# The product of w3 and w_out2 moved between two feed-forwards, its tiles converted in the middle blocks, and the sign merged into a parametric ReLU

## The chip, the core and the metric

The kernel runs on one core of a Trainium2 chip. The metric is the device time of one execution in microseconds, lower is better. TensorE (PE) multiplies, ScalarE (ACT) and VectorE (DVE) work on tiles, GpSimd (POOL) only fills constants here, and SyncE (SP) issues every DMA.

## The reference

A chunked attention is followed by two feed-forwards over 3072 tokens of 512 features:

```
x = attention(q, k, v, mem_k, mem_v)   # chunks of 32 queries, 64 keys each
x = elu(x @ w_in) @ w_out              # w_in 512x2048, w_out 2048x512
h = ((x @ w1) * (x @ w2)) @ w3         # w1, w2 512x1024, w3 1024x1024
out = h @ w_out2                       # w_out2 1024x512
```

q, k and v are float32; the weights are float64 and reach the chip as pairs of 32-bit words.

## The kernel before

Nothing stands between w3 and w_out2, so their product WC (1024x512) is made once on the chip, and the second feed-forward ends in one matmul by WC. Every matmul of the feed-forwards and of WC is done as three (`mm3`, lines 121 to 123), with each operand split into a high half and the rest: a `split` is one cast on ScalarE (line 117) and one subtraction on VectorE (line 118).

**Conversion.** A float64 tile of 128x512 (512 KB) becomes float32 on the chip in a job. `rebase` (line 155, ScalarE) scales the high word as if it were a float32, which moves the exponent. `shift` (159), `sign` (163) and `low` (169) are VectorE instructions on the bits: three places left, the sign put back, the top bits of the low word joined. Then the tile is split into one of 32 weight slots `W`. `Feed.step` issues one stage of each of several jobs, so that one call is about one job's worth of instructions; the letter f in the order strings stands for it. Raw tiles come through four buffers, and at the start through six more that lie where six of the slots will be. There are 72 jobs: 16 of w3, 8 of w_out2, 16 of w_in, 16 of w_out, 8 each of w1 and w2.

**Attention.** 24 groups of 128 queries pass through `plan`, steps 0 to 9: transposes of q and k (`at_turn`, `at_turn2`), scores, maximum and exponential, sum, norm, a flip on VectorE, values, and `at_out`, which splits the result into `xhl`, the input of the first feed-forward. A group begins every 32/3 steps. `at_step`, the letter a, issues the next step. All of it uses the two PSUM banks `PA`. `load_qk` for the next group is issued in step 1 and `load_v` in step 9, on SyncE's queue like every other DMA.

**The order.** It is written out by hand, and each engine executes its instructions in that order. `START` and the loop behind it mix the first 31 attention steps (three groups) with the jobs of w3, w_out2 and w_in 0 to 7 and with the matmuls of WC (`mm_wc`); a job of w3 has two more stages, four transposes on TensorE (`flip`, line 425) and a split from PSUM. WC is stored to DRAM (`wcd`). Then come eight blocks of 384 tokens. A block has 16 iterations of `mm_h` (12 matmuls), `elu_exp` (ReLU and exponential on ScalarE, lines 391 and 392), `mm_x` of two iterations before (12 matmuls), and `elu_split` (lines 398, 117, 118), with two attention steps of the next block's groups in each. In block 0 the rest of the jobs of w_in and w_out stand between them by `IN_BLOCK0`, three steps in two iterations. Blocks 1 to 6 hold no conversion. Block 7 holds no attention, but from its fourth iteration on one conversion step each, for w1 and w2, into slots that the block sets free. The result x1 of a block goes to DRAM (`x1d`) through the tiles `f` and comes back, split, for the second feed-forward.

The second feed-forward has eight blocks of eight iterations: `mm_ab` (24 matmuls), a product on VectorE, and `mm_o` of the iteration before (9 matmuls of 512 columns). In its first block it also finishes the conversion of w1 and w2 and loads a tile of WC per iteration.

Of the kernel before, what the change touches and what calls it, by code (L numbers as in the profile page):

```python
# [19 lines left out]
def tile_kernel(  # L20
# [68 lines left out]
    wcd = [dram.tile([P, 2, DM], F32, name=f"wcd{i}") for i in range(FF2)]  # L89
# [82 lines left out]

    class Job:
        def __init__(self, load, *phases):
            self.load, self.phases = load, ((rebase,), (shift, low), (sign,)) + phases

    class Feed:
# [3 lines left out]
        def __init__(self, jobs, ahead=lambda at: RAWS):  # L181
            self.jobs, self.at, self.loaded, self.ahead = jobs, 0, 0, ahead

        def load(self, n):
            while self.loaded < min(len(self.jobs), n):
                job = self.jobs[self.loaded]
                fn, *args = job.load
                job.raw = fn(*args)
# [12 lines left out]
        def until(self, i):  # L201
            while self.at - len(self.jobs[i].phases) < i:
                self.step()

    def to_slot(slot):
        def fn(job):
            t = W[slot]
            split(t[:, 0, :], t[:, 1, :], job.f)

        return fn  # L210
# [143 lines left out]
    def at_out(G):  # L354
# [6 lines left out]

    plan = [
        (0, at_turn), (1, at_turn2), (1, lambda G: load_qk(G + 1)), (2, at_scores), (3, at_max), (4, at_sum),
        (5, at_norm), (6, at_flip), (8, at_values), (9, at_out), (9, lambda G: load_v(G + 1)),
    ]
    steps = [[] for _ in range(AT_BEFORE + AT_BLOCK * NB)]
    for G in range(NG):
        for at, fn in plan:
            steps[AT_BLOCK * G // GPB + at].append((fn, G))
# [47 lines left out]
    NW3 = 5  # L417
    S_WO2, S_W3T, S_WC = 2 * FF1 - FF2, FF1 - NW3, (FF1 + 3, 2 * FF1 - FF2)

    def wc_job(half, c):  # L420
        slot = S_W3T + (half * FF2 + c) % NW3

        def flip(job):
            for i in range(KT):
                nc.tensor.transpose(PS[4 + c % 2][:, i * P:(i + 1) * P], job.f[:, i * P:(i + 1) * P], ident)

        def back(job):
            t = W[slot]
            split(t[:, 0, :], t[:, 1, :], PS[4 + c % 2])

        return Job((raw_cols, w3[half * KT * P:(half + 1) * KT * P, :], c), (flip,), (back,))

    def mm_wc(half, c, i):
        t, x = W[S_W3T + (half * FF2 + c) % NW3], W[S_WO2 + c]
        ii = slice(i * P, (i + 1) * P)
        mm3(PS[i], t[:, 0, ii], t[:, 1, ii], x[:, 0, :], x[:, 1, :], c == 0, c == FF2 - 1)

    def store_wc(half, i):
        t = W[S_WC[half] + i]
        split(t[:, 0, :], t[:, 1, :], PS[i])  # L440
        stores.append((wcd[half * KT + i], t))

    stores = []

    def store_next():
        if stores:
            o, t = stores.pop(0)
            nc.sync.dma_start(out=o, in_=t.bitcast(F32))
# [49 lines left out]
    with tc.manual_schedule():  # L498
        def weight(i):
            if i < FF1:  # L500
                return Job((raw_cols, w_in, i), (to_slot(i),))
            return Job((raw_rows, w_out, i - FF1, 0), (to_slot(i),))
# [33 lines left out]
        for half in range(2):  # L536
            for c in range(FF2):
# [4 lines left out]
                elif c == SPARE_END:  # L542
                    end_more()
# [122 lines left out]
```

## Time and profile before

| | |
|---|---|
| median of 3 runs | 1182.76 us (1182.22 to 1183.58) |
| the profiled execution's own time | 1183.67 us |
| its span in the trace | 1181.9 us |
| TensorE busy | 1104.5 us, 93% |
| VectorE busy | 532.5 us, 45% |
| ScalarE busy | 435.8 us, 37% |
| DMA moved | 91.06 MB, mean 77 GB/s |

Busy shares are means over the whole span; the stages differ, so they are read stage by stage. Matmuls are pipelined, and a matmul's recorded duration is longer than its distance to the next, so distances between starts are used for TensorE, and for short instructions of the other engines too.

### The profile page before, as it was taken

What the parts mean: (1) busy time and instruction counts of PE and PEld (TensorE: products, weight loads), DVE (VectorE), ACT (ScalarE), POOL (GpSimd) and SP (SyncE); (2) the same over time, 40 slices, a digit from 0 to 9 for tenths busy, and PEclk for the clock granted to TensorE, in tenths of its full rate; (3) what the DMA queues carried; (4) which work ended last, traced back from release to release, by engine and by line L of the source; (5) the groups of instructions that cost most, each with busy time, mean ns of one, the idle gap of its engine ahead of it and who ended that gap; (6) DMA issues with size and microseconds to landing.
All of it is one profiled execution on the core that took longest, in us unless ns stands there. A gap on an engine that the chain in (4) does not pass through costs nothing.

```text
span 1181.9 us, 20762 instructions
## 1 busy us (share of the span) xinstructions
PE 1104.5 (93%) x8800; PEld 1033.9 (87%) x8800; DVE 532.5 (45%) x984; ACT 435.8 (37%) x897; POOL 3.0 (0%) x16
## 2 busy tenths in 40 slices
PE   4768787899999999999999999889999999999998
PEld 3546677899999999999999999889999999999997
DVE  4989778545444444444344445653212212221221
ACT  3554455344434444444335335532212212121211
POOL 1000000000000000000000000000000000000000
PEclk9999888999999999999999999999999999999999
DMA  8955574221221222112212123332100001000000
GB/s 256 279 171 184 152 206 123 54 47 37 63 46 42 72 47 62 37 35 64 52 36 73 25 77 126 129 129 104 54 27 27 28 26 54 24 31 28 1 27 27
DMA packets 143165, 91.06 MB, mean 77 GB/s; under 512 B 102113, under 2 KB 134881, under 8 KB 143073
## 3 DMA queue, kind: packets, MB, share of 16 engines
q1 hardware_dynamic: 143072, 89.74, 26.3%
q8 instruction: 69, 1.13, 0.4%
q14 instruction: 24, 0.19, 0.1%
HBM read 72.94 MB, written 16.78 MB: 76 GB/s over the span
## 4 chain that ended last, share of the span: by engine, by line
PE 78%; DVE 11%; ACT 5%; issue 3%; DMA 2%; SPq 0%; POOL 0%; ACTq 0%; POOLq 0%; DVEq 0%
PE bank L121 21%; PE bank L123 20%; PE bank L122 20%; PE banks L123 4%; PE banks L122 4%; PE banks L121 4%; DVE f L169 2%; PE banks L352 2%; DVE f L163 2%; DVE w L118 2%; DVE f L159 1%; PE banks L294 1%; ACT w L117 1%; ACT eg L392 1%; ACT eg L391 1%
## 5 line engine op out<-in xcount | busy, mean ns | idle before, releaser
L121 PE MATMUL bank<-xhl,w 128*128 128x384 f32 x768 | 266.7, 347 | 5.6 <-DVE eg L398 5.6
L123 PE MATMUL bank<-xhl,w 128*128 128x384 f32 x768 | 260.8, 340 | 0.0
L122 PE MATMUL bank<-xhl,w 128*128 128x384 f32 x768 | 260.6, 339 | 0.0
L117 ACT CAST g<-eg 128x384 fp32r<-128x384 f32 x192 | 98.7, 514 | 287.1 <-DVE eg L398 146.6
L121 PE MATMUL bank<-g,w 128*128 128x384 f32 x512 | 176.3, 344 | 2.8 <-ACT g L117 2.8
L122 PE MATMUL bank<-g,w 128*128 128x384 f32 x512 | 172.6, 337 | 0.3 <-DVE g L118 0.2
L123 PE MATMUL bank<-g,w 128*128 128x384 f32 x512 | 172.4, 337 | 0.0
L118 DVE TENSOR_TENSOR g<-eg,g 128x384 fp32r<-128x384 f32 x192 | 107.2, 558 | 141.7 <-ACT g L117 141.7
L121 PEld LDWEIGHTS bank<-xhl,w 128*128 128x128 f32 x768 | 146.5, 191 | 13.4 <-DVE eg L398 7.8
L479 DVE TENSOR_TENSOR eg<-eg,banks 128x384 f32<-128x384 f32 x64 | 35.5, 555 | 259.0 <-PE banks L123 259.0
L122 PEld LDWEIGHTS bank<-xhl,w 128*128 128x128 f32 x768 | 146.7, 191 | 2.7
L123 PEld LDWEIGHTS bank<-xhl,w 128*128 128x128 f32 x768 | 146.7, 191 | 0.0
L391 ACT ACTIVATE eg<-bank 128x384 f32<-128x384 f32 x128 | 62.8, 490 | 173.9 <-PE bank L123 173.3
L398 DVE SCALAR_TENSOR_TENSOR eg<-eg,bank 128x384 f32<-128x384 f32 x128 | 69.8, 545 | 74.6 <-ACT eg L392 74.6
L121 PEld LDWEIGHTS bank<-g,w 128*128 128x128 f32 x512 | 97.2, 190 | 5.0 <-ACT g L117 3.4
L122 PEld LDWEIGHTS bank<-g,w 128*128 128x128 f32 x512 | 97.3, 190 | 0.8 <-DVE g L118 0.8
L123 PEld LDWEIGHTS bank<-g,w 128*128 128x128 f32 x512 | 97.0, 189 | 0.0
L478 ACT COPY eg<-bank 128x384 f32<-128x384 f32 x64 | 30.8, 481 | 165.6 <-PE bank L123 165.6
L121 PE MATMUL banks<-xhl,w 128*128 128x384 f32 x256 | 85.6, 334 | 0.0
L123 PE MATMUL banks<-xhl,w 128*128 128x384 f32 x256 | 85.5, 334 | 0.0
L122 PE MATMUL banks<-xhl,w 128*128 128x384 f32 x256 | 85.5, 334 | 0.0
L121 PE MATMUL bank<-w,g 128*128 128x512 f32 x192 | 74.8, 390 | 1.4 <-DMA w<-wcd 1.4
(70 smaller groups left out, 1344.4 us busy)
## 6 DMA issues: line engine op xcount, KB each, us to landing
raw<-in_moe_w_dram SPq DMA_DIRECT2D x24, 512.0 KB
raw<-in_moe_w_out_dram SPq DMA_DIRECT2D x20, 512.0 KB
raw<-in_moe_w_in_dram SPq DMA_DIRECT2D x13, 512.0 KB
qn<-in_q_dram SPq DMA_DIRECT2D x24, 256.0 KB
x1d<-st SPq DMA_DIRECT2D x32, 192.0 KB
x<-x1d SPq DMA_DIRECT2D x32, 192.0 KB
out_dram<-st SPq DMA_DIRECT2D x24, 256.0 KB
kn<-in_k_dram SPq DMA_DIRECT2D x20, 256.0 KB
```

The lines of the kernel that those rows point to most:

```text
L117: nc.scalar.copy(hi, src)
L118: nc.vector.tensor_tensor(out=lo, in0=src, in1=hi.bitcast(F32), op=ALU.subtract)
L121: mm(o, lhsT=w_hi, rhs=x_hi, start=start, stop=False)
L122: mm(o, lhsT=w_hi, rhs=x_lo, start=False, stop=False)
L123: mm(o, lhsT=w_lo, rhs=x_hi, start=False, stop=stop)
L163: nc.vector.scalar_tensor_tensor(out=t, in0=h, scalar=-(2 ** 31), in1=t, op0=ALU.bitwise_and, op1=ALU.bitwise_or)
L169: nc.vector.scalar_tensor_tensor(out=t, in0=l, scalar=29, in1=t, op0=ALU.logical_shift_right, op1=ALU.bitwise_or)
L352: mm(o, lhsT=vw[cc, u, 2 * hp + r, :], rhs=pT[cc, r, hp, u, :], start=u == 0, stop=u == 1)
L391: nc.scalar.activation(e, h_t[n], AF.Relu, scale=-1.0)
L398: nc.vector.scalar_tensor_tensor(out=e, in0=e, scalar=-1.0, in1=ph, op0=ALU.add, op1=ALU.max)
L478: nc.scalar.copy(e, pab[0])
L479: nc.vector.tensor_tensor(out=e, in0=e, in1=pab[1], op=ALU.mult)
```

## The change

The jobs of w3, w_out2, w1 and w2 leave the start and block 7. The start now holds the first 31 attention steps and twelve conversion steps, for w_in and w_out alone; block 0 has two steps in each iteration as long as there are any. From group 6 on, each of the 18 remaining attention groups carries one or two jobs of w_out2, w1 and w2, and the first 16 of them also one of w3: rebase, shift and low, and split, in steps of their own. A w3 tile is transposed into `PA` in step 9. Each split tile is stored to DRAM as high and low halves, 512 KB, by the next `at_step`. In block 7 each slot that a matmul has read for the last time is filled again from DRAM, 32 fills; eight more follow during the product. WC is made between the two feed-forwards, 192 matmuls without conversion among them, and stays in slots. `sign` is gone: the rebase is a parametric ReLU with a slope of 2^32 for negative inputs, so that the bit which the shift moves to the top carries the sign. A step now issues high half, shift and low of the next tile, low half, rebase. `at_out` moves from step 9 to step 8. The queries and keys are loaded ahead of the first weights.

```diff
-    RAWS, SPARE, SPARE_JOBS, SPARE_END = 4, (8, 9, 10, 16, 17, 18), 27, 5
-    START = "llikflfafafffafa"
-    IN_WC = (("", "a", "f", "af"), ("f", "a", "f", "a"))
-    AFTER_WC = ("afaa", "aaa")
-    IN_BLOCK0 = (("fa", "a", "f"), ("af", "a", ""))
+    RAWS, SPARE, SPARE_JOBS, SPARE_END = 4, (13, 14, 15, 29, 30, 31), 20, 22
+    START = "ikllll" + 3 * "aafaafaafaafa"
+    IN_BLOCK0 = ("fa", "fa", "")
...
-    wcd = [dram.tile([P, 2, DM], F32, name=f"wcd{i}") for i in range(FF2)]
+    w3d = [[dram.tile([P, 2, 512], F32, name=f"w3d{h}_{c}") for c in range(FF2)] for h in range(2)]
+    wod = [dram.tile([P, 2, 512], F32, name=f"wod{c}") for c in range(FF2)]
+    wabd = [[dram.tile([P, 2, 512], F32, name=f"wabd{c}_{r}") for r in range(2)] for c in range(FF2)]
...
-        nc.scalar.activation(job.f, job.raw[:, :, 1].bitcast(F32), AF.Copy, scale=2.0 ** -112)
+        nc.scalar.activation(job.f, job.raw[:, :, 1].bitcast(F32), AF.Prelu, scale=2.0 ** -112, alpha=2.0 ** 32)
...
-    def sign(job):
-        h, t = job.raw[:, :, 1], job.f.bitcast(I32)
-        nc.vector.scalar_tensor_tensor(
-            out=t, in0=h, scalar=-(2 ** 31), in1=t, op0=ALU.bitwise_and, op1=ALU.bitwise_or
-        )
...
+    def hi_of(job, src=None):
+        nc.scalar.copy(job.to[:, 0, :], job.f if src is None else src)
+    def lo_of(job, src=None):
+        nc.vector.tensor_tensor(
+            out=job.to[:, 1, :], in0=job.f if src is None else src, in1=job.to[:, 0, :].bitcast(F32), op=ALU.subtract
+        )
...
-        def step(self, n=1):
-            for _ in range(n):
-                self.load(self.at + 1)
-                for age, op in ((5, 0), (4, 0), (3, 0), (1, 0), (2, 0), (1, 1), (0, 0)):
-                    i = self.at - age
-                    if 0 <= i < len(self.jobs) and age < len(self.jobs[i].phases):
-                        self.jobs[i].phases[age][op](self.jobs[i])
-                self.at += 1
-                self.load(self.at - 2 + self.ahead(self.at))
+        def do(self, i, *ops):
+            if 0 <= i < len(self.jobs):
+                for op in ops:
+                    op(self.jobs[i])
+        def step(self):
+            i = self.at
+            if i == SPARE_END:
+                end_more()
+            self.load(i + 1)
+            if 0 <= i - 2 < len(self.jobs):
+                self.jobs[i - 2].to = W[self.jobs[i - 2].slot]
+            self.do(i - 2, hi_of)
+            self.do(i - 1, shift, low)
+            self.do(i - 2, lo_of)
+            self.do(i, rebase)
+            self.at += 1
+            self.load(i + RAWS + (len(SPARE) if i + len(SPARE) + RAWS <= SPARE_JOBS else 0))
...
+    mid_jobs, mid_loaded, stores = [], [0], []
+    def mid_load(n):
+        while mid_loaded[0] < min(len(mid_jobs), n):
+            mid_jobs[mid_loaded[0]].fetch()
+            mid_loaded[0] += 1
+    def mid_low(job):
+        shift(job)
+        low(job)
+        mid_load(mid_jobs.index(job) + 3)
+    def mid_split(job, src=None):
+        job.to = pools["st"].tile([P, 2, 512], F32R, tag="st", name="st")
+        hi_of(job, src)
+        lo_of(job, src)
+        stores.append(job)
+    def mid_flip(job):
+        for i in range(KT):
+            nc.tensor.transpose(PA[:, 0, i * P:(i + 1) * P], job.f[:, i * P:(i + 1) * P], ident)
+        mid_split(job, PA[:, 0, :])
+    def store_next():
+        while stores:
+            job = stores.pop(0)
+            nc.sync.dma_start(out=job.store, in_=job.to.bitcast(F32))
     plan = [
         (0, at_turn), (1, at_turn2), (1, lambda G: load_qk(G + 1)), (2, at_scores), (3, at_max), (4, at_sum),
-        (5, at_norm), (6, at_flip), (8, at_values), (9, at_out), (9, lambda G: load_v(G + 1)),
...
+    others = [Job((raw_rows, w_out2, c, 0), store=wod[c]) for c in range(FF2)]
+    others += [Job((raw_cols, (w1, w2)[r], c), store=wabd[c][r]) for c in range(FF2) for r in range(2)]
+    w3s = [Job((raw_cols, w3[h * KT * P:(h + 1) * KT * P, :], c), store=w3d[h][c]) for h in range(2) for c in range(FF2)]
...
+        if G >= GM:
+            n = [(G - GM + i) * n_others // (NG - GM) for i in range(2)]
+            for job, at in zip([others.pop(0) for _ in range(n[1] - n[0])], (0, 6)):
+                mid_jobs.append(job)
+                for i, fn in enumerate((rebase, mid_low, mid_split)):
+                    steps[s0 + at + i].append((fn, job))
+                if at == 0 and w3s:
+                    job = w3s.pop(0)
+                    mid_jobs.append(job)
+                    for at3, fn in ((4, rebase), (5, mid_low), (9, mid_flip)):
+                        steps[s0 + at3].append((fn, job))
...
     def at_step():
         if at_done[0] < min(at_most[0], len(steps)):
+            store_next()
             for fn, G in steps[at_done[0]]:
                 fn(G)
             at_done[0] += 1
...
-    def wc_job(half, c):
-        slot = S_W3T + (half * FF2 + c) % NW3
-        def flip(job):
-            for i in range(KT):
-                nc.tensor.transpose(PS[4 + c % 2][:, i * P:(i + 1) * P], job.f[:, i * P:(i + 1) * P], ident)
-        def back(job):
-            t = W[slot]
-            split(t[:, 0, :], t[:, 1, :], PS[4 + c % 2])
-        return Job((raw_cols, w3[half * KT * P:(half + 1) * KT * P, :], c), (flip,), (back,))
...
+    def wc_bank(half, i):
+        return PS[i] if half else (PS[4], PS[5], PA[:, 0, :], PA[:, 1, :])[i]
...
+    def keep_wc(half, i):
+        s_wc.append(s_w3[half, i])
+        t = W[s_wc[-1]]
+        split(t[:, 0, :], t[:, 1, :], wc_bank(half, i))
+    def fill(slot, src):
+        nc.sync.dma_start(out=W[slot].bitcast(F32), in_=src)
...
-        jobs = []
-        for c in range(FF2):
-            jobs += [wc_job(0, c), Job((raw_rows, w_out2, c, 0), (to_slot(S_WO2 + c),))]
-        for c in range(FF2):
-            jobs += [wc_job(1, c), weight(c)]
-        due = {}
-        order = sorted(range(FF2, 2 * FF1), key=lambda i: i if i < FF1 else i - FF1 + 2)
+                return Job((raw_cols, w_in, i), slot=i)
+            return Job((raw_rows, w_out, i - FF1, 0), slot=i)
+        jobs, due = [], {}
+        order = sorted(range(2 * FF1), key=lambda i: i if i < FF1 else i - FF1 + 2)
         for i in order:
             due[i] = len(jobs)
             jobs.append(weight(i))
...
         run(START)
-        for half in range(2):
-            for c in range(FF2):
-                lead = min(1, 2 * c + 8 * half)
-                feed.until(2 * (half * FF2 + c) + lead)
-                if half == 0:
-                    feed.until(2 * c + 1 + lead)
-                elif c == SPARE_END:
-                    end_more()
-                store_next()
-                last = c == FF2 - 1
-                for i in range(KT):
-                    mm_wc(half, c, i)
-                    if last:
-                        store_wc(half, i)
-                    if not last:
-                        run(IN_WC[half][i])
-                if last:
-                    run(AFTER_WC[half])
...
+                store_next()
+                mid_ctx.close()
                 at_ctx.close()
                 late = ctx.enter_context(tc.tile_pool(name="late", bufs=1, side="right"))
-                pools["raw"] = ctx.enter_context(tc.tile_pool(name="raw2", bufs=RAWS, side="right"))
-                freed = []
-                for m in range(FF1 + 2):
-                    freed += [m] if m < FF1 else []
-                    freed += [FF1 + m - 2] if m >= 2 else []
-                s_ab, s_wc, jobs = {}, [], []
-                for c in range(FF2):
-                    for r, src in enumerate((w1, w2)):
-                        s_ab[c, r] = freed.pop(0)
-                        jobs.append(Job((raw_cols, src, c), (to_slot(s_ab[c, r]),)))
-                    s_wc.append(freed.pop(0))
-                feed = Feed(jobs)
+                ab_jobs = [(c, r) for c in range(FF2) for r in range(2)]
...
+                mid_ctx = ExitStack()
+                pools["raw"] = mid_ctx.enter_context(tc.tile_pool(name="raw2", bufs=2, side="right"))
+                pools["st"] = mid_ctx.enter_context(tc.tile_pool(name="st_p", bufs=2, side="right"))
+                mid_load(2)
...
                 if j == 0:
-                    run(IN_BLOCK0[f % 2][0])
+                    run(IN_BLOCK0[0])
                 else:
                     at_step()
-                    if j == NB - 1 and f >= 3:
-                        feed.step()
...
                 if j == 0:
-                    run(IN_BLOCK0[f % 2][1])
+                    run(IN_BLOCK0[1])
...
-                run(IN_BLOCK0[f % 2][2])
-            if j == 0 and f >= 3:
-                store_next()
+                run(IN_BLOCK0[2])
+            if n >= NH - FF1:
+                free = [f] if n < NH else []
+                if n >= NH - FF1 + 2:
+                    free.append(FF1 + n - 2 - (NH - FF1))
+                for slot in free:
+                    if len(s_wo) < FF2 and len(s_wo) <= len(s_w3):
+                        fill(slot, wod[len(s_wo)])
+                        s_wo.append(slot)
+                    elif len(s_w3) < 2 * FF2:
+                        half, c = divmod(len(s_w3), FF2)
+                        fill(slot, w3d[half][c])
+                        s_w3[half, c] = slot
+                    else:
+                        c, r = ab_jobs.pop(0)
+                        fill(slot, wabd[c][r])
+                        s_ab[c, r] = slot
...
+        store_x1(NB - 1)
+        for half in range(2):
+            for c in range(FF2):
+                for i in range(KT):
+                    mm_wc(half, c, i)
+                    if c == FF2 - 1:
+                        keep_wc(half, i)
+            for i in range(KT, FF2):
+                c, r = ab_jobs.pop(0)
+                fill(s_w3[half, i], wabd[c][r])
+                s_ab[c, r] = s_w3[half, i]
...
-            if j == 0 and f < FF2:
-                feed.until(2 * f + 1)
             if n < NA:
                 mm_ab(n)
-                if j == 0:
-                    nc.sync.dma_start(out=W[s_wc[f]].bitcast(F32), in_=wcd[f])
-                    feed.step()
```

## Rows read from the trace of the kernel before

**Rows 1.** Windows: engines' busy us by stage, granted clock, DMA share, GB/s.
```profile
0.00:113.50 113.50, 72.66 (x676) 55.15 (x677) 92.15 (x172) 52.83 (x96) 2.99 (x16) 0.95 0.76 226
113.50:231.70 118.20, 94.24 (x829) 89.25 (x827) 85.19 (x158) 59.60 (x124) 0.00 (x0) 0.88 0.46 131
231.70:701.30 469.60, 468.06 (x4820) 448.94 (x4819) 210.58 (x391) 197.30 (x425) 0.00 (x0) 1.00 0.20 49
701.30:772.90 71.60, 65.84 (x364) 63.09 (x363) 43.69 (x82) 36.94 (x75) 0.00 (x0) 0.99 0.44 144
772.90:1181.90 409.00, 403.67 (x2120) 377.50 (x2118) 100.87 (x185) 89.12 (x183) 0.00 (x0) 1.00 0.12 41
```

**Rows 2.** Waits of TensorE in 0 to 113.5: us in total, times, longest.
```profile
PE bank L425 <- DVE f L163: 25.8, 10, 5.4
PE banks L267 <- DMA qn<-in_q_dram: 10.7, 1, 10.7
```

**Rows 3.** Timeline of ScalarE, block 0: first and last of its 16 line-391 ReLUs.
```profile
115.82 0.49 ACT L391 ACTIVATE eg<-bank 128x384 f32<-128x384 f32 x1 [0.71 <-PE bank L123]
...
219.44 0.48 ACT L391 ACTIVATE eg<-bank 128x384 f32<-128x384 f32 x1
```

**Rows 4.** Timeline of ScalarE, block 7: ReLUs without, then with a conversion step.
```profile
713.30 0.49 ACT L391 ACTIVATE eg<-bank 128x384 f32<-128x384 f32 x1 [1.98 <-PE bank L123]
...
717.46 0.49 ACT L391 ACTIVATE eg<-bank 128x384 f32<-128x384 f32 x1 [1.98 <-PE bank L123]
...
746.95 0.48 ACT L391 ACTIVATE eg<-bank 128x384 f32<-128x384 f32 x1
...
751.68 0.48 ACT L391 ACTIVATE eg<-bank 128x384 f32<-128x384 f32 x1
```

**Rows 5.** Timeline of VectorE: one conversion step's instructions at the start.
```profile
42.56 0.68 DVE L118 TENSOR_TENSOR w<-f,w 128x512 fp32r<-128x512 f32 x1
43.16 0.42 DVE L159 TENSOR_SCALAR f<-f 128x512 int32<-128x512 int32 x1
43.49 0.68 DVE L163 SCALAR_TENSOR_TENSOR f<-raw,f 128x512 int32<-128x512 int32 x1
44.09 0.68 DVE L169 SCALAR_TENSOR_TENSOR f<-raw,f 128x512 int32<-128x512 int32 x1
44.70 0.42 DVE L159 TENSOR_SCALAR f<-f 128x512 int32<-128x512 int32 x1
```

**Rows 6.** Groups by line and form, VectorE's two ELU instructions: busy, mean ns.
```profile
L118 DVE TENSOR_TENSOR g<-eg,g 128x384 fp32r<-128x384 f32 x192 | 107.2, 558 | 141.7 <-ACT g L117 141.7
L398 DVE SCALAR_TENSOR_TENSOR eg<-eg,bank 128x384 f32<-128x384 f32 x128 | 69.8, 545 | 74.6 <-ACT eg L392 74.6
```

**Rows 7.** Windows: the stretch of the first three attention groups, all engines.
```profile
12.70:104.70 92.00, 64.07 (x637) 48.01 (x637) 80.80 (x151) 45.34 (x85) 0.00 (x0) 0.94 0.76 233
```

**Rows 8.** Groups by line and form, ScalarE: the rebase, and the table load.
```profile
L155 ACT ACTIVATE f<-raw 128x512 f32<-128x512 f32 x57 | 38.4, 674 | 17.2 <-DMA raw<-in_moe_w_out_dram 5.9 <-DMA raw<-in_moe_w_dram 4.2 <-DVE f L169 3.6
L155 ACT ACT_TABLE_LOAD x1 | 1.3, 1283 | 0.7 <-PEq L650 0.7
```

**Rows 9.** Timeline of TensorE: four transposes of w3, then product matmuls.
```profile
100.71 0.66 PE L425 MATMUL bank<-ident,f 128*128 128x128 f32 x4 [0.68 <-DVE f L163]
101.12 0.47 PE L121 MATMUL bank<-w,w 128*128 128x512 f32 x1
101.43 0.39 PE L122 MATMUL bank<-w,w 128*128 128x512 f32 x1
...
103.72 0.39 PE L123 MATMUL bank<-w,w 128*128 128x512 f32 x1
```

**Rows 10.** Windows of VectorE: the first attention group (clock, DMA share, GB/s last).
```profile
12.70:42.10 29.40, 24.49 (x47) 0.94 0.99 324
```

**Rows 11.** Timeline of SyncE: output stores of the second feed-forward's first two blocks.
```profile
830.95 1.54 SPq L495 DMA_DIRECT2D out_dram<-st  x3
...
881.08 1.53 SPq L495 DMA_DIRECT2D out_dram<-st  x3
```

More of the change, by code (lines that the diff above doesn't have):

```diff
@@ L171, in low, with __init__, fetch @@
         )
-    class Job:
-        def __init__(self, load, *phases):
-            self.load, self.phases = load, ((rebase,), (shift, low), (sign,)) + phases
+    def hi_of(job, src=None):
[4 more added lines that the diff above has]
+        )
+    class Job:
+        def __init__(self, load, slot=None, store=None):
+            self.load, self.slot, self.store = load, slot, store
+        def fetch(self):
+            fn, *args = self.load
+            self.raw = fn(*args)
@@ L177, in tile_kernel, with __init__ @@
     class Feed:
-        def __init__(self, jobs, ahead=lambda at: RAWS):
-            self.jobs, self.at, self.loaded, self.ahead = jobs, 0, 0, ahead
+        def __init__(self, jobs):
+            self.jobs, self.at, self.loaded = jobs, 0, 0
         def load(self, n):
             while self.loaded < min(len(self.jobs), n):
-                job = self.jobs[self.loaded]
-                fn, *args = job.load
-                job.raw = fn(*args)
+                self.jobs[self.loaded].fetch()
                 self.loaded += 1
-        def step(self, n=1):
-            for _ in range(n):
-                self.load(self.at + 1)
-                for age, op in ((5, 0), (4, 0), (3, 0), (1, 0), (2, 0), (1, 1), (0, 0)):
-                    i = self.at - age
-                    if 0 <= i < len(self.jobs) and age < len(self.jobs[i].phases):
-                        self.jobs[i].phases[age][op](self.jobs[i])
-                self.at += 1
-                self.load(self.at - 2 + self.ahead(self.at))
+        def do(self, i, *ops):
+            if 0 <= i < len(self.jobs):
+                for op in ops:
+                    op(self.jobs[i])
@@ L201, in until @@
         def until(self, i):
-            while self.at - len(self.jobs[i].phases) < i:
+            while self.at - 3 < i:
                 self.step()
-    def to_slot(slot):
-        def fn(job):
-            t = W[slot]
-            split(t[:, 0, :], t[:, 1, :], job.f)
-        return fn
     e_t, q_t, k_t, qT_t, kT_t, pT_t = {}, {}, {}, {}, {}, {}
@@ L362, in tile_kernel @@
+    def mid_flip(job):
[6 more added lines that the diff above has]
+            nc.sync.dma_start(out=job.store, in_=job.to.bitcast(F32))
     plan = [
         (0, at_turn), (1, at_turn2), (1, lambda G: load_qk(G + 1)), (2, at_scores), (3, at_max), (4, at_sum),
[L364 removed]
+        (5, at_norm), (6, at_flip), (8, at_values), (8, at_out), (9, lambda G: load_v(G + 1)),
@@ L365, in tile_kernel @@
     ]
+    GM = 2 * GPB
     steps = [[] for _ in range(AT_BEFORE + AT_BLOCK * NB)]
+    others = [Job((raw_rows, w_out2, c, 0), store=wod[c]) for c in range(FF2)]
+    others += [Job((raw_cols, (w1, w2)[r], c), store=wabd[c][r]) for c in range(FF2) for r in range(2)]
+    w3s = [Job((raw_cols, w3[h * KT * P:(h + 1) * KT * P, :], c), store=w3d[h][c]) for h in range(2) for c in range(FF2)]
+    n_others = len(others)
     for G in range(NG):
+        s0 = AT_BLOCK * G // GPB
         for at, fn in plan:
-            steps[AT_BLOCK * G // GPB + at].append((fn, G))
+            steps[s0 + at].append((fn, G))
+        if G >= GM:
[9 more added lines that the diff above has]
+                        steps[s0 + at3].append((fn, job))
@@ L370, in tile_kernel @@
+    assert not others and not w3s
     at_done, at_most = [0], [AT_BEFORE]
@@ L413, in store_x1 @@
             nc.sync.dma_start(out=x1d[j][:, o, :], in_=t[:, 0:TB])
-    NW3 = 5
-    S_WO2, S_W3T, S_WC = 2 * FF1 - FF2, FF1 - NW3, (FF1 + 3, 2 * FF1 - FF2)
-    def wc_job(half, c):
-        slot = S_W3T + (half * FF2 + c) % NW3
-        def flip(job):
-            for i in range(KT):
-                nc.tensor.transpose(PS[4 + c % 2][:, i * P:(i + 1) * P], job.f[:, i * P:(i + 1) * P], ident)
-        def back(job):
-            t = W[slot]
-            split(t[:, 0, :], t[:, 1, :], PS[4 + c % 2])
-        return Job((raw_cols, w3[half * KT * P:(half + 1) * KT * P, :], c), (flip,), (back,))
+    s_w3, s_wo, s_ab, s_wc = {}, [], {}, []
+    def wc_bank(half, i):
+        return PS[i] if half else (PS[4], PS[5], PA[:, 0, :], PA[:, 1, :])[i]
     def mm_wc(half, c, i):
-        t, x = W[S_W3T + (half * FF2 + c) % NW3], W[S_WO2 + c]
+        t, x = W[s_w3[half, c]], W[s_wo[c]]
         ii = slice(i * P, (i + 1) * P)
[L436 to L448, printed above, removed]
+        mm3(wc_bank(half, i), t[:, 0, ii], t[:, 1, ii], x[:, 0, :], x[:, 1, :], c == 0, c == FF2 - 1)
+    def keep_wc(half, i):
[4 more added lines that the diff above has]
+        nc.sync.dma_start(out=W[slot].bitcast(F32), in_=src)
     x1_t = {}
@@ L513, in tile_kernel @@
             jobs.append(weight(i))
-        feed = Feed(jobs, lambda at: RAWS if at >= SPARE_JOBS - 6 else min(RAWS + at // 2, RAWS + len(SPARE) - 1))
+        feed = Feed(jobs)
         def run(what):
```

4 lines of the change are left out of this document (1 added, 3 removed).

## The prediction

> **What bounds the kernel now.** I read the stages first, by cutting the span where the code changes phase [rows 1]. Up to 113.5 us the attention of the first three groups runs together with the conversion of w3, w_out2 and half of w_in, and their product is made. Block 0 fills 113.5 to 231.7, blocks 1 to 6 fill 231.7 to 701.3, block 7 ends at 772.9, and the second feed-forward takes the rest. The reader is to see that TensorE is busy for 99.7% of the middle and 99% of the end, but only for 72.7 of 113.5 us at the start and 94.2 of 118.2 us in block 0, where VectorE has 92.2 and 85.2 us of work.
>
> Then the waits of TensorE. At the start the largest is 25.8 us for line 163, the sign instruction, in front of the transposes of w3; 10.7 us go to the first q [rows 2]. In blocks 1 to 6 TensorE is idle for 1.5 of 469.6 us [rows 1]. So the start and block 0 are bound by conversion, and everything behind them by TensorE. Work of TensorE that moves from the start to the end is paid in full there; conversion that moves into the middle is paid only where it disturbs TensorE.
>
> Block 0 needs one more view. Its sixteen iterations follow each other in 6.91 us (first and last ReLU, 103.62 us over 15 intervals) [rows 3]; the middle's take 469.6/96 = 4.89 us. VectorE is busy for 72% of block 0, so throughput alone is not what limits it. Block 7 shows the mechanism, without attention: iterations without a conversion step take 4.16 us, with one step 4.73 us [rows 4]. TensorE's work is the same. ScalarE and VectorE execute in order, and an iteration's cast must wait for the VectorE pieces queued ahead of it, while the next ReLU stands behind that cast: a ring. One old step costs VectorE shift 0.33, sign 0.60, low 0.61 and the low half of the split 0.60, start to start, 2.14 us in all [rows 5]. The check: block 0 has 1.5 steps in an iteration and 1.09 us of attention (the middle's VectorE time of 210.6 us, less 96 times 0.545 + 0.558 us [rows 6], leaves 5.8 us a group, and an iteration holds two of a group's 10.67 steps). 4.73 + 0.5 x 2.14 + 1.09 = 6.89 us, against 6.91 measured. I trust this ring for the sum.
>
> **The change, part by part.**
>
> *Start.* Before, attention and conversion share 12.7 to 104.7 us, of which VectorE is busy 80.8 [rows 7]. Attention's part is 3 x 5.8 = 17.4, so conversion has 63.4, and 28.6 us remain without it. The new start does twelve steps of three instructions, 12 x 1.54 = 18.5 us (two of the pieces of the pipeline's start fall away; I leave them in). Simply added, that is 47 us. But less conversion also covers less of attention's legs on TensorE and ScalarE. If the dead time of 92.0 - 80.8 = 11.2 us doubles, it is 58. I take 49, near the lower end, as the steps stand between the legs. Attention can begin earlier: q no longer stands behind two weight tiles, 1.05 MB at the start's 226 GB/s [rows 1], 4.6 us; against that the first rebase waits for a tile now issued after q, k and v, and it stands ahead of the first exponential on ScalarE. I take 9 us for the begin. First matmul of block 0: 9 + 49 = 58 us, from 56 to 67.
>
> *Block 0.* The start leaves twelve of 34 steps done, so eleven iterations hold two steps and the others none. The sign instruction is gone. The order inside a step changes too: shift and low of one tile run before the low half of another, and so while ScalarE is still at ReLU, exponential and high half. From the ring of 4.73 I take out shift, sign and low (1.54), and add a second new step (1.54) and attention (1.09): 5.8 us. I take 6.0; the ends are TensorE's 4.89 and the old 6.9. Six further iterations up to the first store of x1 take 4.89. 11 x 6.0 + 6 x 4.89 = 95.3 us, and block 0 ends at 153.3 instead of 231.7: **-78.4**.
>
> *ScalarE's new function.* The trace shows the rebase as a scaled copy of 0.67 us and a single table load of 1.283 us in the whole program [rows 8]; it shows no parametric ReLU. The lower bound of what it costs beyond that is nothing (the same 0.67 us, no load); the upper is two loads around each rebase that stands between exponentials. I take nothing, since ReLU, Exp and Copy alternate there without a second load. The Trainium skill, "ScalarE: Activation LUTs", section "Table sets: the hidden batching unit", says that cheap functions stand in every table set but does not name this one among them; the single load beside Copy, ReLU and Exp agrees for those three, and no run here shows it for the fourth. The same page's section "What ACT_TABLE_LOAD costs" puts a switch at about 2.66 us with its drain; by that the 28 loads of the rival below would cost 74 us instead of 36.
>
> *Middle.* Forty tiles (8 of w_out2, 16 of w1 and w2, 16 of w3) are converted in 18 groups, stored and read back. VectorE has 210.6 of 469.6 us and gets 40 x 1.54 = 62 more; it has room. The 16 transposes of w3, four instructions each, are TensorE work: 0.41 us [rows 9], 6.6 us. They write the bank that the next group's first transposes need one step later; one group in three comes that close. For such waits I take 3 us. Bounds: 0 above the 6.6, and 40 x 0.57 = 23 us if each job lengthens its iteration as a step does in block 7. I stay near the lower end, as the product of an iteration is not needed until two iterations later and only 40 of 96 have a job. On SyncE's queue every raw load waits for a low just issued, every store for a split; q, k and v of the next group stand behind them, but have eight steps (some 20 us). The store of x1 finds one of four f buffers held by a job, so its fourth copy waits for the first copy's DMA; VectorE stands then, ahead of an ELU product that has two iterations. Nothing for either; without that cover, some 3 us in each of six blocks. **+9.6**.
>
> *Block 7.* No steps remain: 16 x 4.16 = 66.6 for 71.6, **-5.0**. Instead 32 fills of 0.52 MB run, 16.8 MB in 66.6 us, 252 GB/s; the start reached 324 GB/s at a DMA share of 0.99 [rows 10], so they fit, and the last eight are not read until 44 us later.
>
> *Product.* 192 matmuls of 512 columns at 0.229 us (ten intervals from 101.43 to 103.72) [rows 9]: **+44.0**. Its first half uses banks that are free; its last splits hide behind the first 24 matmuls of the next phase. If not, 2 us.
>
> *Second feed-forward.* Its first block takes 58.0 us to its store (from 772.9 to 830.95); at the later pace of 50.13 [rows 11], with one more mm_ab of 4.16, 54.3. The conversion and the late reads of wcd that cost the difference are gone: **-3.7**.
>
> Sum: -78.4 + 9.6 - 5.0 + 44.0 - 3.7 = -33.5, a span of 1148.4 us. The profiled execution took 1183.67, 1.8 more than its span and 0.9 more than the median, so the forecast is **1149 us**.
>
> **The rivals.**
>
> *Block 0 keeps its pace.* VectorE's work per iteration barely falls (1.5 x 2.14 against 2 x 1.54), and ScalarE's rises by half a step. Against it: VectorE waits for ScalarE's high half less. At 6.9 us, with a start at 62, block 0 ends at 167: 1163.
>
> *The middle loses its steady state.* For it speaks block 7's 0.57 us a step; against it the slack. 23 for 9.6: 1163; both together 1177.
>
> *Slower: ScalarE reloads tables.* If the new function is not loaded together with the exponential, the start takes up to 6 loads, block 0 two in each of eleven iterations, inside the ring: 28 x 1.283 = 36 us, which alone uses up the gain (26 loads on the path decide). The middle would take 80 more, 103 us of ScalarE, of which I put 30 on the path: 1215. For it: the trace has no such function. Against it: three functions share one load.
>
> *Fills come late.* TensorE would wait for w3 or w_out2 in the product. The rate above speaks against it; 10 us, 1159.
>
> **How the numbers follow.** Forecast 0.60; block 0's pace 0.15; the middle 0.11; both 0.04; tables 0.08; fills 0.02. The measurement tells 0.2%, 2.4 us, from no change. Faster: forecast, the two single rivals and fills, 0.88. Both together end close enough to the old time to count 0.03 as same and 0.01 as slower; with the tables, slower is 0.09. The low end takes the ends 56, 4.89 and 6.6 (block 0 ends at 139): 1132. The high end covers either single rival and stops at 1175, short of both together; tables are left out.
>
> **What would show it.** Right: one table load; the first matmul of block 0 near 58 us and the first store of x1 near 153; ReLUs about 6 us apart, then 4.9; store to store in the middle 78.3 to 80 us; block 7 at 67; 192 wide matmuls in 44 without gaps. Wrong would be: a row of table loads; ReLUs 7 us apart after the start; waits of TensorE for VectorE's low halves in the middle, or for DMA in the product.

## The result and the profile after

The changed kernel takes 1150.72 us (median of 4 runs, 1149.34 to 1151.27) where the kernel before took 1182.83 in the same comparison: ratio 0.9726, 95% interval 0.971 to 0.9743. The forecast was 1149. The profiled execution of the changed kernel has a span of 1148.6 us, 33.3 less than before; the forecast for that difference was 33.5.

The stages of the changed kernel, by windows (columns as in [rows 1]: PE, PEld, DVE, ACT, POOL busy, clock, DMA share, GB/s):

```profile
0.00:59.90 59.90, 17.59 (x421) 14.78 (x421) 33.98 (x63) 22.34 (x44) 2.99 (x16) 1.00 0.86 238
59.90:159.20 99.30, 89.58 (x835) 84.70 (x836) 70.08 (x130) 58.10 (x120) 0.00 (x0) 0.97 0.40 111
159.20:634.50 475.30, 474.82 (x4876) 454.91 (x4875) 274.70 (x511) 236.33 (x503) 0.00 (x0) 1.00 0.45 135
634.50:698.90 64.40, 64.40 (x372) 64.31 (x372) 20.67 (x39) 25.88 (x52) 0.00 (x0) 1.00 0.86 280
698.90:1148.60 449.70, 444.40 (x2303) 411.13 (x2301) 94.87 (x173) 88.60 (x180) 0.00 (x0) 1.00 0.12 38
```

Against [rows 1] the start is 53.6 us shorter, block 0 18.9, block 7 7.2; the middle is 5.7 longer and everything behind block 7 40.7, where the product now stands. VectorE works 274.7 of 475.3 us in the middle, 64 more than before, and TensorE is still busy throughout: the trace records no wait of TensorE there at all.

The ReLUs of block 0, on ScalarE's timeline (first, third, twelfth and last of 16; compare [rows 3]), and the first stores of x1 and of the output on SyncE's (compare [rows 11]):

```profile
64.53 0.49 ACT L447 ACTIVATE eg<-bank 128x384 f32<-128x384 f32 x1 [4.70 <-PE bank L124]
...
71.41 0.52 ACT L447 ACTIVATE eg<-bank 128x384 f32<-128x384 f32 x1
...
128.62 0.49 ACT L447 ACTIVATE eg<-bank 128x384 f32<-128x384 f32 x1
...
147.11 0.49 ACT L447 ACTIVATE eg<-bank 128x384 f32<-128x384 f32 x1 [1.59 <-PE bank L124]
```

```profile
159.17 1.02 SPq L469 DMA_DIRECT2D x1d<-st  x2
...
797.64 1.54 SPq L536 DMA_DIRECT2D out_dram<-st  x3
```

The second entry of `IN_BLOCK0` stands behind `mm_x`, and the first two iterations have no `mm_x`: they hold one conversion step each, and ten iterations behind them hold two. On VectorE the nine intervals from the third to the twelfth ReLU hold two each, 57.21 us or 6.36 each, and VectorE is busy for 49.7 of them:

```profile
71.41:128.62 57.21, 49.41 (x497) 46.67 (x496) 49.67 (x92) 36.79 (x75) 0.00 (x0) 0.94 0.50 142
```

They are not alike: the shortest takes 4.94 us and the longest 7.68, according to the attention steps in them. The two intervals before them take 6.88 together, and the four behind them 4.62 each.

ScalarE's groups by line and form (compare [rows 8]):

```profile
L157 ACT ACTIVATE f<-raw 128x512 f32<-128x512 f32 x60 | 40.2, 670 | 1.4 <-DMA raw<-in_moe_w_out_dram 0.7 <-DMA raw<-in_moe_w_in_dram 0.7
...
L279 ACT ACT_TABLE_LOAD x1 | 1.3, 1283 | 0.7 <-PEq L682 0.7
```

The parametric ReLU takes 670 ns, the scaled copy took 674, and there is still one table load. The Trainium skill, "ScalarE: Activation LUTs", section "Table sets: the hidden batching unit", puts cheap functions into every set and does not name this one among them; the trace shows that it too runs beside Exp, ReLU and Copy without a second load.

### The profile page after: what moved, and what is told of

Read it like the earlier page. It is cut to its first block, busy times and chain, and to the rows that moved or that the text cites. A ratio compares the mean times of both kernels' runs of the same rounds, so it can differ in the third digit from the quotient of the medians.

```text
span 1148.6 us, 20849 instructions
## 1 busy us (share of the span) xinstructions
PE 1090.8 (95%) x8800; PEld 1029.8 (90%) x8800; DVE 494.3 (43%) x912; ACT 431.2 (38%) x897; POOL 3.0 (0%) x16
## 4 chain that ended last, share of the span: by engine, by line
PE 82%; DVE 7%; ACT 4%; DMA 3%; issue 2%; SPq 0%; POOL 0%; DVEq 0%; POOLq 0%
PE bank L122 22%; PE bank L124 21%; PE bank L123 21%; PE banks L122 4%; PE banks L124 4%; PE banks L123 4%; PE banks L360 2%; DMA vw<-in_v_dram 2%; PE banks L302 1%; DMA qn<-in_q_dram 1%; ACT g L118 1%; DVE eg L454 1%; DVE w L173 1%; DVE f L165 1%; PE banks L275 1%
## 5 line engine op out<-in xcount | busy, mean ns | idle before, releaser
L122 PEld LDWEIGHTS bank<-g,w 128*128 128x128 f32 x512 | 96.1, 188 | 1.4
L123 PEld LDWEIGHTS bank<-g,w 128*128 128x128 f32 x512 | 96.2, 188 | 0.0
L124 PEld LDWEIGHTS bank<-g,w 128*128 128x128 f32 x512 | 96.1, 188 | 0.0
L454 DVE SCALAR_TENSOR_TENSOR eg<-eg,bank 128x384 f32<-128x384 f32 x128 | 69.7, 545 | 53.6 <-ACT eg L448 53.6
```

What stands on the lines that cost most here:

```text
L122: mm(o, lhsT=w_hi, rhs=x_hi, start=start, stop=False)
L123: mm(o, lhsT=w_hi, rhs=x_lo, start=False, stop=False)
L124: mm(o, lhsT=w_lo, rhs=x_hi, start=False, stop=stop)
L454: nc.vector.scalar_tensor_tensor(out=e, in0=e, scalar=-1.0, in1=ph, op0=ALU.add, op1=ALU.max)
```

## The experiments

The stages of all runs, each from its profiled execution, by the first matmul of block 0, the first stores of x1 of each block and the first store of the output (us; the rest, some 351 us, is alike in all). "Product" is the stretch from block 7's store to the first store of the output.

| | start | block 0 | blocks 1-6 | block 7 | product and first output | median |
|---|---|---|---|---|---|---|
| before | 113.5 | 118.2 | 469.6 | 71.6 | 58.0 | 1182.83 |
| changed | 59.9 | 99.3 | 475.3 | 64.4 | 98.8 | 1150.72 |
| changed, sign back | 63.7 | 111.4 | 488.4 | 64.4 | 98.7 | 1179.31 |
| changed, low half first | 63.0 | 117.5 | 475.2 | 64.4 | 98.7 | 1172.10 |
| changed, without both | 69.0 | 133.1 | 488.8 | 64.4 | 98.8 | 1206.07 |
| changed, middle dearer | 59.0 | 98.4 | 515.9 | 64.4 | 98.8 | 1189.48 |
| changed, six steps at start | 53.9 | 108.1 | 475.6 | 64.4 | 98.8 | 1153.31 |
| changed, at_out in step 9 | 59.1 | 100.0 | 511.7 | 64.4 | 98.8 | 1187.50 |
| changed, no transposes in the middle | 59.2 | 99.5 | 466.3 | 64.4 | 98.8 | 1141.06 |
| changed, a quarter of the product | 59.2 | 100.0 | 475.5 | 64.4 | 66.1 | 1117.76 |
| before, merge | 98.1 | 109.6 | 469.5 | 66.5 | 58.6 | 1156.91 |
| before, merge and order | 93.0 | 100.3 | 469.6 | 63.0 | 58.5 | 1138.31 |
| the same, at_out in step 8 | 100.1 | 93.6 | 466.6 | 62.9 | 54.9 | 1132.30 |

The kernel before was run beside each set and had medians of 1183.6 to 1184.5 there, so differences between sets of under 2 us are not read. Intervals of a few runs are given where a verdict hangs on them.

**The sign as an instruction again.**

```diff
-            self.do(i - 1, shift, low)
+            self.do(i - 1, shift, sign, low)
...
+        sign(job)
         low(job)
         mid_load(mid_jobs.index(job) + 3)
```

with Copy in place of the parametric ReLU.

> The changed kernel with the sign as an instruction of VectorE of its own again (scaled copy, shift, sign, low), in every job. The ring theory (block 0 is set by the work that ScalarE and VectorE execute in order for one iteration, and the middle has slack): eleven iterations with two steps grow by 2 x 0.6 = 1.2 us each, 13 us, the twelve steps of the start cost 4 to 7 us, the middle nothing: 1167 to 1171 us, with the ReLUs of block 0 about 7.1 us apart. The rival that block 0 waits for attention's round trips and not for VectorE's instruction count: under 5 us, 1151 to 1156. The rival that the middle stands at its edge: 24 us more there, 1190 or above.

28.6 us more. The start grew by 3.8 and block 0 by 12.1, as the ring has it: the nine intervals with two steps grew by 1.25 us each, to 7.61, where 1.2 was forecast. But the middle grew by 13.1, which it did not allow for: not the 24 of the rival either. TensorE's waits in this run's blocks 1 to 6 (total, times, longest):

```profile
PE banks L366 <- DVE pT L355: 5.0, 6, 0.8
PE banks L398 <- DVE xhl L119: 3.3, 5, 0.7
PE bank L122 <- DVE eg L461: 0.9, 2, 0.5
PE banks L281 <- DVE st L179: 0.5, 3, 0.2
```

The reader is to see who waits: the values matmul for the flip on VectorE two steps earlier, and the transposes of w3 for `at_out`. Those are attention's own hand-overs, one iteration apart at most. The ELU product (line 461), on whose two iterations I had counted, makes 0.9 us of 9.7 here; with a still dearer middle, below, it makes the most. The other 3 us of the growth are in no recorded wait, and the granted clock of that stretch is 1.00, so they are not the clock's.

**The low half ahead of shift and low.**

```diff
-            self.do(i - 1, shift, low)
-            self.do(i - 2, lo_of)
+            self.do(i - 2, lo_of)
+            self.do(i - 1, shift, low)
```

> The changed kernel with one thing of the step's order put back: the low half of a tile is issued right behind its high half, ahead of shift and low of the next tile. No instruction is added. The ring theory: shift and low of one step no longer run while ScalarE is at ReLU, exponential and high half; 0.94 us in each of eleven iterations, 10 us, and a few in the start: 1160 to 1165. The rival that only the number of instructions counts: no difference, 1150 to 1153.

21.4 us more, without an added instruction; the rival falls. Block 0 alone gives 18.2; each of the nine intervals with two steps grew by 1.51 us and not by 0.94. VectorE's timeline in one iteration of this run, and then in the same iteration of the changed kernel, shows why:

```profile
116.35 0.69 DVE L173 TENSOR_TENSOR w<-f,w 128x512 fp32r<-128x512 f32 x1 [0.90 <-ACT w L170]
116.96 0.42 DVE L161 TENSOR_SCALAR f<-f 128x512 int32<-128x512 int32 x1
117.41 0.69 DVE L165 SCALAR_TENSOR_TENSOR f<-raw,f 128x512 int32<-128x512 int32 x1
118.79 0.69 DVE L173 TENSOR_TENSOR w<-f,w 128x512 fp32r<-128x512 f32 x1 [0.69 <-ACT w L170]
```

```profile
104.15 0.68 DVE L173 TENSOR_TENSOR w<-f,w 128x512 fp32r<-128x512 f32 x1
104.75 0.42 DVE L161 TENSOR_SCALAR f<-f 128x512 int32<-128x512 int32 x1
105.21 0.69 DVE L165 SCALAR_TENSOR_TENSOR f<-raw,f 128x512 int32<-128x512 int32 x1
105.82 0.68 DVE L173 TENSOR_TENSOR w<-f,w 128x512 fp32r<-128x512 f32 x1
```

VectorE stands for ScalarE's high half at both steps, 0.90 and 0.69 us, and in the changed kernel at neither; I had put the wait into the ring once.

One rival was not in any forecast: TensorE's granted clock. In block 0 its mean is 0.88 in the kernel before [rows 1], 0.97 in the changed kernel and 0.91 in this run, so some matmuls run at the lower of its two levels, 1.2 instead of 2.4 GHz. Two intervals of this run with the same instructions of VectorE (the second is the one shown) settle it for this run:

```profile
76.04:82.73 6.69, 6.11 (x95) 5.70 (x94) 4.46 (x8) 3.98 (x10) 0.00 (x0) 1.00 0.88 250
114.77:121.46 6.69, 6.69 (x90) 6.16 (x89) 4.47 (x8) 4.00 (x10) 0.00 (x0) 0.74 1.01 221
```

The granted clock is 1.00 in one and 0.74 in the other, and both take 6.69 us: TensorE is not what sets their pace. The run without both parts, below, has such a pair too, 8.75 us at 1.00 and at 0.80. In the kernel before the intervals do not repeat in this way, so how much of its 118.2 us in block 0 is the clock's was not separated.

**Both taken out: the move alone.** The sign is back and the low half comes first.

```diff
-            self.do(i - 1, shift, low)
-            self.do(i - 2, lo_of)
+            self.do(i - 2, lo_of)
+            self.do(i - 1, shift, sign, low)
```

> The changed kernel without both of its cheap parts: the sign as an instruction of its own and the low half right behind the high half, as before; only the move of the conversions and of the product is left. The theory now: each part is paid where ScalarE and VectorE execute in order, so the costs of the first two runs add: 28.6 + 21.4 us, 1200 us, slower than before by 1.5%; block 0 with its first store of x1 near 197 us and the middle near 489 us. The rival that the two parts share one wait: less than the sum, 1179 to 1190.

1206.07, ratio to the kernel before 1.0176 (1.0159 to 1.0193): slower by 1.8%. The two costs add, with 5 us on top, all of them before the first store of x1 (202.1 us); the middle is at 488.8. So the move loses 22 us, and that with `at_out` in step 8 and the queries loaded first, which this run keeps.

**The merge alone, on the kernel before.**

```diff
-            self.load, self.phases = load, ((rebase,), (shift, low), (sign,)) + phases
+            self.load, self.phases = load, ((rebase,), (shift, low), (lambda job: None,)) + phases
```

with the parametric ReLU in `rebase`.

> The kernel before with the merge of the sign alone: the rebase is the parametric ReLU, the sign instruction is gone, and nothing is moved. If VectorE's work sets the start and block 0, as I argued, the start loses up to 36 x 0.6 = 21 us and block 0 0.9 us in each of some 15 iterations, 14 us, block 7 and the first block of the second feed-forward some 5: as far down as 1143 us, which would make the merge alone worth more than the whole change. If the move carries the gain and the start is also bound by attention's chain and by the product's waits, 15 us at most: 1168 or above.

1156.91, 27 us less than before, between the two cases: the start gives 15.4 of the 21, block 0 8.6 of the 14, block 7 5.1. The second case is ruled out: the start was bound by VectorE's instructions enough for most of the merge to be won there.

**Merge and order, on the kernel before.** The stages of a job stay where they are; the split is issued in two parts.

```diff
-                for age, op in ((5, 0), (4, 0), (3, 0), (1, 0), (2, 0), (1, 1), (0, 0)):
+                for age, op in ((4, 0), (3, 0), (1, 0), (1, 1), (4, 1), (3, 1), (0, 0)):
...
     def to_slot(slot):
+        return halves(slot, lambda job: job.f)
```

where `halves` returns the cast on ScalarE and the subtraction on VectorE as two operations.

> The kernel before with both cheap parts and without the move: parametric ReLU, no sign, and in each step the high half first, then shift and low of the next tile, then the low half. If the order of a step is worth as much here as in the changed kernel for each step that block 0 holds (23 of 22), some 15 to 20 us below the merge alone: 1137 to 1142, better than the changed kernel by 10 us, and the move would not be worth making. If the start's VectorE, which is full there, gains nothing from an order and only block 0 does (15 iterations with 0.6 to 0.9 us): 1143 to 1148. If the order only helps two steps in one iteration: 1152 to 1157.

1138.31, ratio 0.9616 (0.9596 to 0.9636), the first case. Without the move, the two cheap parts give 46 us, and the changed kernel with the move on top is 12 us slower. By stages, the move saves 33.1 us in the start and 1.0 in block 0 and pays 5.7 in the middle, 1.4 in block 7 and 40.3 for the product and what stands with it.

**And at_out in step 8, on the same.**

```diff
-        (5, at_norm), (6, at_flip), (8, at_values), (9, at_out), (9, lambda G: load_v(G + 1)),
+        (5, at_norm), (6, at_flip), (8, at_values), (8, at_out), (9, lambda G: load_v(G + 1)),
```

The empty stage of the sign is taken out of a job as well.

> The kernel before with merge and order as in the last run but one, with at_out in step 8 too, and with the empty stage taken out that the sign had left in a job. If the waits of TensorE for the low half of at_out (6.1 us in that run) and the length of a job's pipeline stood on the path: 4 to 8 us, 1130 to 1134. If the start is bound by VectorE's count and by attention: 1136 to 1140.

1132.30, ratio 0.9567 (0.9549 to 0.9585): the best of all runs. Its middle (columns as above), and TensorE's largest wait over the whole span:

```profile
193.70:660.30 466.60, 466.60 (x4819) 449.19 (x4819) 210.59 (x391) 197.45 (x424) 0.00 (x0) 1.00 0.20 49
```

```profile
PE bank L431 <- DVE f L169: 18.3, 11, 2.7
```

The middle is 3.0 us shorter than before [rows 1]. It holds no conversion, so that is `at_out`. In the kernel before TensorE's only recorded wait there is for the low half of `at_out`, 1.5 us in all, and here there is none:

```profile
PE banks L267 <- DVE xhl L118: 1.5, 6, 0.3
```

Behind block 7 the first output comes 3.6 us sooner. The start and block 0 together do not change (193.3 and 193.7): what the shorter job moves from one to the other cancels. Which of the two edits does that was not separated. The start is still held by VectorE in front of the transposes of w3. With `at_out` in step 8 on both sides, the changed kernel is 18 us slower than this one.

**The middle made dearer.**

```diff
         low(job)
+        low(job)
...
         lo_of(job, src)
+        hi_of(job, src)
+        lo_of(job, src)
```

> The changed kernel with the middle blocks' conversion made dearer and the same result: low is issued twice, high and low half twice, so a job costs VectorE 2.74 us instead of 1.54 and ScalarE some 0.5 us more. If the conversion in the middle is hidden by the two iterations of slack: 0 to 4 us, 1150 to 1155. If the middle is just at its edge: 40 x 0.6 to 40 x 1.2 us, 1175 or above.

38.8 us more, all of it in the middle, 1.0 us a job: the middle is at its edge. VectorE's busy share in it, by the window of this run, is 64%:

```profile
157.50:673.40 515.90, 484.97 (x4878) 457.85 (x4877) 329.33 (x591) 256.44 (x543) 0.00 (x0) 1.00 0.41 125
```

TensorE's waits in it (total, times, longest):

```profile
PE bank L122 <- DVE eg L457: 11.5, 16, 2.3
PE banks L275 <- DVE st L173: 8.3, 6, 1.5
PE banks L394 <- DVE xhl L119: 6.7, 5, 1.3
PE banks L360 <- DVE pT L349: 4.2, 5, 0.9
```

The largest is for the ELU product (line 457): the two iterations that were to hide the conversion are used up.

**at_out back in step 9.**

```diff
-        (5, at_norm), (6, at_flip), (8, at_values), (8, at_out), (9, lambda G: load_v(G + 1)),
+        (5, at_norm), (6, at_flip), (8, at_values), (9, at_out), (9, lambda G: load_v(G + 1)),
```

> The changed kernel with at_out back in step 9, the step in which a w3 tile is transposed into the same banks. If the one step of distance is what keeps TensorE from waiting: 16 flips wait for a cast and a subtraction, 0.6 to 1.3 us each, 10 to 20 us in the middle: 1160 to 1171. If the middle's queue absorbs it: 1150 to 1153.

36.8 us more, 36.4 in the middle, nearly twice the upper case. TensorE's one recorded wait there, for line 391, the transposes of w3:

```profile
PE banks L391 <- DVE xhl L119: 25.7, 11, 2.3
```

They now stand directly behind `at_out` on the same banks. Each of the eleven waits takes 2.3 us. Nearly all of the other 11 us go with the granted clock. Here are the middle, one of the waits, and what follows it:

```profile
159.10:670.80 511.70, 485.76 (x4877) 463.86 (x4876) 275.81 (x511) 237.82 (x503) 0.00 (x0) 0.98 0.42 126
437.30:439.68 2.38, 0.04 (x2) 0.01 (x1) 0.69 (x1) 1.49 (x3) 0.00 (x0) 1.00 0.40 89
439.68:443.10 3.42, 3.42 (x14) 3.42 (x15) 1.15 (x2) 0.59 (x1) 0.00 (x0) 0.57 0.14 57
```

Behind this wait, and behind five others of the eleven, the granted clock falls for a few microseconds, here to a mean of 0.57, so most of this stretch is at the lower level. Over the middle, in windows of 5 us, the share by which the clock falls short of 1.00, times the length, adds up to 10.2 us; TensorE is busy for 10.9 us longer than in the changed kernel. In the changed kernel's middle the clock stays at 1.00.

**No transposes in the middle.**

```diff
-        for i in range(KT):
-            nc.tensor.transpose(PA[:, 0, i * P:(i + 1) * P], job.f[:, i * P:(i + 1) * P], ident)
-        mid_split(job, PA[:, 0, :])
+        mid_split(job)
```

> The changed kernel without the transposes of w3 in the middle blocks; the tile is split as it is, so w3 stands there untransposed. If the 5.7 us that the middle grew are TensorE's 64 transposes, 16 x 0.41 = 6.6 us: blocks 1 to 6 fall to 469 to 470 us, 1144 to 1145 in all. If it is the conversion on VectorE and ScalarE: no change, 1150.

Blocks 1 to 6 fall to 466.3, further than expected, and the time to 1141.06. The transposes cost 9.0 us, of which 6.6 are TensorE's own by [rows 9]; no recorded wait shows the rest, and where it lies stays open. Without them the forty conversions are hidden to the last: 466.3 is the middle of the run with `at_out` in step 8 and no conversion, 466.6.

**A quarter of the product.**

```diff
                 for i in range(KT):
-                    mm_wc(half, c, i)
+                    if c in (0, FF2 - 1):
+                        mm_wc(half, c, i)
```

> The changed kernel with 144 of the product's 192 matmuls left out (only the first and the last of eight terms of each sum are made). If TensorE pays the product in full between the feed-forwards: 144 x 0.229 = 33.0 us less, 1117.7. If something else, the fills from DRAM or the splits, sets the length of that stretch: less than 25 us.

1117.76, 33.0 us less: the product between the feed-forwards is paid at TensorE's rate, and the fills and splits do not set the length of that stretch.

**Fewer steps at the start.**

```diff
-    START = "ikllll" + 3 * "aafaafaafaafa"
+    START = "ikllll" + "aaf" + 3 * "aaaaaf" + "aaaaaaf" + "aaaaaf"
```

> The changed kernel with six conversion steps at the start instead of twelve, each right behind the second transposes or the flip of a group, where VectorE waits for TensorE and ScalarE; block 0 holds two steps in fourteen iterations instead of eleven. If the start is a chain of attention into which steps are pressed: its three groups fall from 17.4 us to about 15, 6 to 8 us, block 0 gives 3 us back: 1145 to 1148. If the steps of the start are hidden already: 3 us slower, 1153 to 1155.

1153.31. The start did fall by 6.0, as the chain of attention would have it, but block 0 grew by 8.8 and not by 3: its 15 intervals from the first to the last ReLU take 6.04 us each. A step costs at least as much in block 0 as in the start.

## Why the prediction was right, point by point

- **Block 0 as a ring.** 5.8 by the sum, 6.0 taken, 6.36 measured where two steps stand in an iteration. The mechanism holds: taking out either cheap part lengthened these intervals, by 1.25 and 1.51 us. Two things were off. The count: I put two steps into eleven iterations, but it is ten with two and the first two with one. And the worth of the order inside a step: VectorE's wait for the high half stands at nearly every step, not at one of two. The check on the kernel before, 6.89 against 6.91, compares a mean over intervals from 5.0 to 9.3 us, so its closeness proves less than I took it for.
- **Start.** 58 us forecast, 59.9 measured; the first transposes at 8.1 us, where they waited for the first q until 10.7 before [rows 2]; what loading the queries first is worth was not tested by itself. The three groups take some 17 us each, the chain of attention more than VectorE's sum.
- **End of block 0.** 153.3 forecast, 159.2 measured. Part of it is a slow beginning, which I had not priced: TensorE comes out of a start in which it was busy for 17.6 of 59.9 us, and the first matmuls of block 0 follow each other in 0.32 us, three in 0.96, where a few microseconds later three take 0.52. TensorE's timeline, and the window of the slow matmuls:

```profile
61.41 0.52 PE L122 MATMUL bank<-xhl,w 128*128 128x384 f32 x1
...
62.37 0.52 PE L122 MATMUL bank<-xhl,w 128*128 128x384 f32 x1
...
66.19 0.33 PE L122 MATMUL bank<-xhl,w 128*128 128x384 f32 x1
...
66.71 0.60 PE L275 MATMUL banks<-ident,qn 128*128 128x128 f32 x4
```

```profile
59.90:64.80 4.90, 4.86 (x14) 4.46 (x15) 1.68 (x3) 0.27 (x1) 0.00 (x0) 1.00 0.43 95
```

  The granted clock recorded there is 1.00, the upper level of 2.4 GHz, so the trace does not show these matmuls as throttled, although their pace is near half; the reason stays open. It costs some 2 us.

- **Middle.** +9.6 forecast, +5.7 measured, and here the reason was wrong though the size was near. I said that two iterations of slack hide the conversion. There is hardly any: 0.6 us more of VectorE in a job costs 13 us, and 1.2 us with half a microsecond of ScalarE costs 41. What brought the middle home is `at_out` in step 8, an edit that I listed and gave no price. In the kernel before it makes the middle 3.0 us shorter, and in the changed kernel it keeps the transposes of w3 from costing 36 more. That the number came near is luck.
- **Block 7.** -5.0 forecast, -7.2 measured. Between the two stores stand 31 groups of twelve matmuls and not 32, 64.5 us at 2.08 each.
- **Product.** +44.0 - 3.7 = 40.3 forecast, 40.7 measured, and the quarter of the product shows the rate. Block 7 moved 280 GB/s, and no fill was late. The banks of the first half were not all free, though: TensorE's only recorded wait in this stretch is for the split out of the first bank of `PA`, before the last sum goes into the second:

```profile
720.97 0.50 PE L122 MATMUL banks<-w,w 128*128 128x512 f32 x1 [1.40 <-DVE w L119]
```

- **The rivals.** No table is loaded a second time. Block 0 did not keep its pace. The middle's steady state held, but by less than I thought: with the sign unmerged, or `at_out` left where it was, that rival would have been the result.
- **The errors.** 5.9 us too few up to the end of block 0, 3.9 and 2.2 too many after it, 0.4 too few at the product: they cancel to 0.2, and that they do is luck.

What the prediction did not ask is which part carries the gain. It credits the move with the start, and the move does empty it; but the product has to be paid elsewhere, where TensorE has no gaps left. The merge and the order inside a step carry the gain, on either kernel.

## What to carry to other kernels

Before work is moved out of a stage bound by VectorE, shorten that work and reorder it so that no engine waits for the instruction issued just before on another one: here that was worth 46 us where it stood, and the move on top of it cost 12, or 18 with `at_out` in step 8 on both sides. When several edits come together, price each against the kernel without the others; a sum that comes out right does not tell which of them pays.
An engine that is busy for 58% of a stage need not have room, even where the engine that bounds the stage has no recorded wait: test it by issuing an instruction twice. And a short wait of TensorE can cost more than itself: the granted clock behind it tells.

## What was not expected

That a change of one step in the place of one split (`at_out`, 24 times in the program) is worth 36 us in one kernel and 3 in the middle of the other. And that taking out 64 transposes of 0.1 us each gave back 9.0 us where their own time is 6.6.
